# A fused attention and long-convolution kernel: a new written order of steps, PSUM pools and copy engines

## The chip, the core and the metric

The kernel runs on one core of a Trainium2 chip. Its time is device microseconds of one launch, taken by the device. The core's engines work beside each other, each through its own queue in order: TensorE (PE, with its weight loads as PEld), VectorE (DVE), ScalarE (ACT), GpSimd (POOL) and SyncE (SP), which here issues nearly all DMA transfers. A profile comes from one execution of its own, whose time can differ from the median of the timed runs.

## The reference

Two independent parts share the sequence length S = 2048 and the width D = 576; their outputs stand side by side in 1152 columns, all in bf16.

```python
# part A: dilated sliding attention, H = 32 heads of 18 columns, window W = 8, dilation 2
qkv = x @ wqkv                                  # [2048, 3*576]
logits[h, s, w] = q[h, s] . k[h, s - 2*w] / sqrt(18)     # -1e9 where s - 2*w < 0
attn = softmax(logits over w)
o[h, s] = sum_w attn[h, s, w] * v[h, s - 2*w]
a = o @ wo
# part B: short and long convolution (H3)
k_shift = sum_t shift(k, t) * shift_k[:, t]     # 4 taps
kv = k_shift * v
y = irfft(rfft(kv, 4096) * rfft(ssm_k, 4096))[:2048] + kv * ssm_D
out = concat(a, q * y)
```

## The kernel before

Part A keeps x, q, k and v transposed, so heads lie on partitions. Part B does the long transform in two matmul stages with a transposition through DRAM between them: stage one writes `Dx` (from kv) and `Dk` (from the filter), stage two reads them back in eight groups (two halves of the columns, four groups of rows), multiplies the spectra, inverts, writes `Dy`, and a last stage reads `Dy`.

Nothing schedules this program at run time. One string, `ORDER`, lists 405 steps, and a loop (last lines of the kernel function) calls the function of each step in turn, so each engine's queue holds its instructions in just this order. A step's letter after the colon picks a PSUM pool (`a` or `b`, two buffers each) and the engine of the copy out of PSUM (`s`: ACT, L103; `v`: DVE, L105). Without a letter the step's default holds; a `ys` without `s` multiplies straight out of PSUM on DVE. Before an instruction the tile framework puts the waits its data need. Each SP transfer also waits for the one about eight places ahead of it to land, since eight semaphores go round.

The steps, with their functions' lines:

| step | what it does |
|---|---|
| `lx` L234, `lwq`, `lwt`, `lwv` L247-L258 | load x in half quarters (288 KB each), and the weights |
| `lk` L241, `lv` L238, `ld` L268 | load k in four chunks (`lk.0` also two halo pieces), v in four, ssm_D |
| `lkn` L260, `kw` L264, `kt` L476 | load the filter by DMA transpose into a ring of seven, write it as rows to `Kt`, read it back in eight pieces |
| `tj`, `t0` to `t5`, `tv`, `tw` L284-L358 | constants; `t3` ends in a sine on ACT that `tw` on DVE needs |
| `wm` L291 | eleven matmuls on zeros |
| `ia`, `ib` L411, L423; `im` L416 | transposed tables by DMA; a negated table by a copy |
| `xt` L365, `sk` L445 | transpose x on PE; spread the four taps over partitions |
| `qk` L395, `qt` L401, `wt` L442 | projections for q and k; their tails; a copy of weight columns |
| `cv` L453 | short convolution on DVE, eight instructions per chunk (L455, L461, L468) |
| `sx`, `kp` L426 | stage one of kv and filter: two matmuls, a copy, and after each third two stores to `Dx` or `Dk` |
| `v` L379 | v projection, 40 matmuls |
| `lm` L484, `lb` L493 | products q times shifted k on DVE; sum over a head's columns on PE |
| `sm` L512 | softmax in two halves |
| `kl`, `xl` L546, `ks`, `xs` L536 | load and transform one group |
| `gp` L559, `gi` L568 | spectrum product on DVE; inverse on PE, then a POOL store to `Dy` |
| `pm` L584, `ps` L591 | weights times shifted v on DVE; their sum on PE |
| `po` L622, `pz` L627 | output projection; `pz` holds the last two `ps` |
| `yl` L635, `ql` L639, `ys` L643 | load `Dy` and q, last transform, product, store |

Intermediate results live in rings that a step takes a slot from and a later one gives back. The full products of `lm` have three slots; `lb.n` gives two back:

```python
prr = Ring(*[mk.take(2, S) for _ in range(3)])                         # L224
nc.vector.tensor_tensor(prr.get((n, h)), q2[h], k2[h][...], ALU.mult)   # L487, lm.n.h
prr.drop((n, 0)); prr.drop((n, 1))                                      # end of lb.n
```

The output stages of `ys` have two slots (L229), the loaded groups four (L216).

Of the kernel before, what the change touches and what calls it, by code (L numbers as in the profile page):

```python
# [15 lines left out]


ORDER = """
tj lx.0.0 lx.0.1 lx.2.0 lwq.1.0 lx.1.0 lx.2.1 lwt lx.1.1 lwq.1.1 lwq.0.1 tv lk.0 lx.3.0 t2 sk.0:a t0 lk.2 sk.2:bv
lx.3.1 sk.1:b xt.0.1:bs xt.0.0:as xt.0.2:bs wm.11:a xt.2.2:as t3 xt.1.2:bs xt.1.0:as qk.1.0.0:b lk.1 xt.2.1:as  # L20
xt.1.1:as xt.2.0:bs t1 tw lwq.0.0 cv.0.0 cv.0.1 t4 qk.1.1.0:b wt qk.1.1.1:a t5 lv.0 lwv lkn.8 lkn.2 lkn.12 lkn.9 lk.3
lkn.13 lkn.4 qk.1.1.2:b xt.3.2:bs qk.0.1.0:a cv.0.3 lkn.6 xt.3.1:bs lkn.7 cv.0.4 lkn.5 lv.1 kw.6 cv.0.2 cv.0.5
xt.3.0:as cv.1.4 cv.0.6 cv.1.0 qk.0.0.2:b cv.1.1 kw.4 lkn.10 cv.0.7 kw.3 qk.0.1.2:b cv.1.3 lkn.14 qk.0.0.1:a sx.0.0:a
sx.0.1:b cv.3.3 cv.1.2 qk.1.1.3:b lkn.15 lkn.0 sx.0.2:a cv.1.5 sx.1.0:a lkn.11 qk.0.1.3:b cv.3.4 sx.1.1:b qt.3:a lkn.1
sx.1.2:b cv.2.1 kw.7 lkn.3 ld qk.0.1.1:a qt.0:b cv.1.6 cv.2.3 kw.0 kw.5 cv.2.4 cv.1.7 qk.0.0.3:b cv.2.0 cv.2.2
sx.2.0:a cv.2.5 kw.2 kw.1 qt.2:b cv.3.5 sx.2.1:a cv.2.6 sx.2.2:b kt.0 cv.3.1 qk.1.0.2:a sx.3.0:b sx.3.1:a kt.1
sx.3.2:b cv.3.0 qt.1:a qk.0.0.0:b qk.1.0.1:a qk.1.0.3:b kp.0.0:a lv.2 cv.3.2 lm.0.2 cv.3.6 kp.0.1:b lm.6.2 lv.3
kp.0.2:a lm.6.1 kp.1.0:b lm.6.0 cv.2.7 kp.1.1:b kp.1.2:a lm.0.0 v.4:a lb.6:a kt.3 kt.2 sx.4.0:b sx.4.1:a lm.0.1 lm.7.0
ia.3 sx.4.2:a sx.5.0:b sx.5.1:b v.2:a ia.5 lb.0:a ia.1 sx.5.2:b kp.2.0:b kt.4 cv.3.7 kp.2.1:a vz kp.2.2:a kt.7 lm.7.1
ia.0 lm.1.0 v.7:b lb.7:b lm.4.1 sx.6.0:a ib sx.6.1:a sx.6.2:b v.1:b sx.7.0:a lm.1.1 sx.7.1:b lm.2.2 sx.7.2:b lb.1:a  # L30
ia.2 lm.4.2 kp.7.0:a lm.4.0 kp.7.1:b xl.3 kp.7.2:b lm.2.1 v.5:a lb.4:b kt.6 kp.3.0:b lm.2.0 kp.3.1:a lm.3.0 kp.3.2:b
im.0 v.3:a kt.5 xl.5 lb.2:b kp.4.0:a kp.4.1:b kp.4.2:b lm.3.1 xl.6 im.1 v.6:a lb.3:a ia.7 kp.6.0:a kp.6.1:b lm.5.0
kp.6.2:a kp.5.0:b lm.5.1 lb.5:av kp.5.1:a sm.1.0 sm.1.1 kp.5.2:b sm.1.2 sm.1.3 xs.5.0:a sm.1.4 xs.3.0:bv ia.4 sm.0.0
v.0:a vh.1 sm.0.1 sm.1.5:a sm.0.2 xs.5.1:a sm.0.3 sm.0.4 xs.3.1:b v.8:a sm.1.6 pm.1.0 pm.1.6 kl.3 sm.0.5:a ps.1.0:b
ks.3.0:a pm.1.3 vh.0 ks.3.1:b gp.3.0 kl.5 gp.3.1 sm.0.6 ps.1.6:a kl.2 ks.5.0:b ks.5.1:a ps.1.3:b pm.0.0 lwo.0 xl.2
kl.0 ks.2.0:a vh.2 ks.2.1:b ia.6 xl.0 lwo.3 gi.3.0:a gi.3.1:b ps.0.0:a gp.5.0 xs.2.0:b gi.5.0:a gp.5.1 pm.1.1 gi.5.1:b
gp.2.0 pm.1.4 xs.2.1:b gp.2.1 ks.0.0:a pm.0.3 xs.6.0:b xl.1 gi.2.0:a ks.0.1:b kl.6 ql.1 xs.0.0:a xs.0.1:b kl.1 lwo.1
gp.0.0 gi.2.1:a ps.1.1:b gp.0.1 ps.0.3:a pm.0.8 xs.1.0:b pm.0.7 gi.0.0:a ks.6.0:b xs.6.1:a kl.7 ps.1.4:bv gi.0.1:a
ks.1.0:b pm.0.1 ks.6.1:a gp.6.0 xl.4 ps.0.7:b gp.1.0 ps.0.8:b ql.3 pm.0.4 xs.1.1:a ks.1.1:b gi.6.0:a ps.0.1:b kl.4
gi.1.0:a gp.6.1 gp.1.1 pm.1.5 pm.0.6 ks.7.0:b xl.7 ql.2 lwo.2 xs.4.0:a gi.1.1:b ps.0.4:a ql.0 ks.4.0:b gi.6.1:a pm.0.5  # L40
xs.7.0:b ps.1.5:av xs.7.1:b ks.7.1:a yl.2 xs.4.1:b ps.0.5:a ps.0.6:b gp.7.0 ks.4.1:a yl.3 yl.1 gi.7.0:b gp.4.0
gi.4.0:a pm.0.2 gp.4.1 yl.0 ps.0.2:b gp.7.1 gi.4.1:a gi.7.1:bv ys.2.0:as ys.2.1:b ys.3.0:as ql.4 ys.3.1:a pm.1.2 yl.4
ql.7 po.0.0.0:v pm.1.8 yl.7 pm.1.7 po.0.1.0 ps.1.2:a ys.0.0:bs ys.0.1:as po.0.0.1:v yl.6 pz.1.0.0 ys.4.0:as ql.6
ys.4.1:as ys.1.0:bs ys.1.1:a ql.5 yl.5 po.1.0.1:v po.1.1.0 ys.7.0:b ys.6.0:as ys.7.1:as ys.6.1:b po.1.1.1:v po.0.1.1
ys.5.0:a ys.5.1:bs
"""


# [654 lines left out]
```

## Time and profile before

| | |
|---|---|
| runs, median (lowest to highest) | 210.17 us (209.7 to 215.51), 3 runs |
| the profiled execution | 211.04 us, span 209.1 us |
| busy in the span | PE 185.2 us (89%), PEld 118.3 (57%), DVE 177.8 (85%), ACT 160.7 (77%), POOL 12.9 (6%) |
| transfers | 56.20 MB, mean 269 GB/s |
| chain that ended last | PE 46%, ACT 27%, DMA 16%, issue 6%, DVE 2% |
| granted TensorE clock | full in all 40 slices |

Busy shares are means over stretches with different limits: PE is nearly always busy in the first 60 us and in the last 35, DVE from 15 to 170 us, ACT most between 105 and 170. Line L103 is the copy helper on ACT, used by nearly every step, so rows are told apart by tile and shape. A row of a window gives the busy time of each engine in it, with the number of instructions in brackets. In a group's row, the numbers behind the bar are the busy time of the group, the mean duration of one in ns, and the idle time of its engine just before, with what ended most of it.

### The profile page before, as it was taken

The numbers are of one execution on the slowest core, as the hardware profiler recorded it, in microseconds if no ns is written. First come the engines' busy times: TensorE is split into PE (matmuls) and PEld (weight loads), VectorE is DVE, ScalarE is ACT, GpSimd is POOL, SyncE is SP. The second block draws the span as 40 slices with busy tenths as digits, with TensorE's granted clock in tenths as the row PEclk, the third lists the DMA queues.
The fourth block names the chain that finished last, engine by engine and source line by source line (L and its number), as shares of the span: only waits on it lengthen the run. The fifth ranks groups of instructions, "written<-read, shape, count | busy, mean of one in ns | idle before, by whom it ended". The sixth has DMA issues, their size and how long they took to land.

```text
span 209.1 us, 6223 instructions
## 1 busy us (share of the span) xinstructions
PE 185.2 (89%) x2645; PEld 118.3 (57%) x2645; DVE 177.8 (85%) x157; ACT 160.7 (77%) x244; POOL 12.9 (6%) x39
## 2 busy tenths in 40 slices
...
GB/s 162 317 316 396 239 211 158 311 198 299 275 368 247 260 181 261 241 214 367 261 250 226 264 242 240 310 350 246 256 390 246 179 330 377 248 335 304 223 314 135
DMA packets 66797, 56.20 MB, mean 269 GB/s; under 512 B 16673, under 2 KB 60306, under 8 KB 66770
## 3 DMA queue, kind: packets, MB, share of 16 engines
...
q8 instruction: 20, 0.33, 0.7%
...
q10 hardware_dynamic: 2, 0.00, 0.0%
...
## 4 chain that ended last, share of the span: by engine, by line
PE 46%; ACT 27%; DMA 16%; issue 6%; DVE 2%; SPq 0%; ACTq 0%; DVEq 0%
ACT area L103 24%; PE psB L377 8%; PE psA L377 5%; DMA Dx<-area 5%; PE psA L610 5%; DMA out_dram<-area 4%; DMA Dy<-area 4%; PE psA L384 3%; PE psA L576 3%; PE psB L599 3%; PE psB L432 2%; DMA Dk<-area 2%; PE psA L599 2%; PE psA L432 2%; DMA area<-in_B_shift_k_dram 2%
## 5 line engine op out<-in xcount | busy, mean ns | idle before, releaser
L103 ACT ACTIVATE area<-psA 128x576 bf16<-128x576 f32 (+7 forms) x117 | 83.5, 757 | 33.1 <-PE psB L610 15.0
L103 ACT ACTIVATE area<-psB 128x576 bf16<-128x576 f32 (+5 forms) x113 | 80.2, 757 | 7.9 <-PE psB L377 4.0
L588 DVE TENSOR_TENSOR area<-area,area 128x4096 bf16<-128x4096 bf16 x18 | 40.6, 2284 | 0.9 <-DMA area<-area 0.8
L487 DVE TENSOR_TENSOR area<-area 128x4096 bf16<-128x4096 bf16 x16 | 35.8, 2286 | 1.0 <-PE psA L504 0.7
L377 PEld LDWEIGHTS <-area 128*128 128x128 bf16 x160 | 15.5, 98 | 17.5
L377 PE MATMUL psB<-area,area 128*128 128x512 bf16 x100 | 23.1, 379 | 0.0
L563 DVE TENSOR_TENSOR area<-area 128x2304 bf16<-128x2304 bf16 x16 | 21.1, 1351 | 1.3 <-ACT area L103 1.0
L461 DVE TENSOR_TENSOR area<-area,area 128x2304 bf16<-128x2304 bf16 x16 | 21.0, 1348 | 0.0
L541 PEld LDWEIGHTS <-W 128*64 128x64 bf16 x256 | 14.0, 108 | 12.3 <-issue 11.1
L610 PE MATMUL psA<-area,area 32*128 32x288 bf16 x288 | 18.7, 281 | 1.6 <-ACT area L103 1.1
L610 PE MATMUL psB<-area,area 32*128 32x288 bf16 x288 | 18.7, 281 | 0.0
L384 PEld LDWEIGHTS <-area 128*32 128x32 bf16 x360 | 15.2, 142 | 5.6 <-issue 2.8
L599 PEld LDWEIGHTS <-ident 64*64 64x64 bf16 x576 | 15.3, 106 | 5.1 <-issue 3.5
L610 PEld LDWEIGHTS <-area 32*128 32x128 bf16 x576 | 15.5, 93 | 4.6 <-issue 2.2
L384 PE MATMUL psA<-area,area 128*32 128x512 bf16 x280 | 16.7, 384 | 0.4 <-ACT area L103 0.2
L432 PEld LDWEIGHTS <-T 128*128 128x128 bf16 x96 | 8.6, 97 | 14.6 <-issue 9.3
L541 PE MATMUL psB<-area,W 128*64 128x288 bf16 x152 | 14.7, 290 | 1.8 <-ACT area L103 1.1
L455 DVE TENSOR_TENSOR area<-area,area 128x2304 bf16<-128x2304 bf16 x12 | 15.8, 1350 | 0.1
L576 PEld LDWEIGHTS <-IAt 64*128 64x128 bf16 x256 | 12.4, 94 | 5.8 <-issue 1.5
L432 PE MATMUL psB<-area,T 128*128 128x384 bf16 x52 | 12.6, 326 | 3.5 <-ACT area L103 3.5
L377 PE MATMUL psA<-area,area 128*128 128x512 bf16 x60 | 13.9, 379 | 0.0
L576 PE MATMUL psA<-area,IAt 64*128 64x288 bf16 x176 | 13.0, 283 | 0.4
...
## 6 DMA issues: line engine op xcount, KB each, us to landing
...
```

Source lines behind the costliest of these rows:

```text
L103: nc.scalar.activation(dst, src, ACT.Copy, **({} if scale is None else {"scale": scale}))
L377: nc.tensor.matmul(ps[:, u, :], w[:, kb, cols[u]:cols[u] + 128], xT[:, j, kb], start=(kb == 0), stop=(kb == 4))
L384: nc.tensor.matmul(ps[32 * a:32 * a + 32, u, :], wv[:, kb, 2 * n + u:D:DH], xT[:, a, kb], start=(kb == 0), stop=(kb == 4), tile_position=( ...
L432: nc.tensor.matmul(ps[:, ri, 0:384], T1[:, ri, :], sf[:, 384 * ch:384 * ch + 384], start=True, stop=not extra)
L461: nc.vector.tensor_tensor(dst, kfull[:, 4 * c + 3 - j:4 * c + 7 - j, :], skb[:, j, :].unsqueeze(1).to_broadcast([128, 4, D]), ALU.mult)
L487: nc.vector.tensor_tensor(prr.get((n, h)), q2[h], k2[h][:, :, o0:o0 + S], ALU.mult)
L541: nc.tensor.matmul(ps[64 * hp:64 * hp + 64, im, 0:HD], W2[:, im, 8 * g + 2 * prl + hp].rearrange("p l f -> p (l f)"), Wt[:, 2 * prl + hp, ...
L563: nc.vector.tensor_tensor(Pv, Xv.unsqueeze(2).to_broadcast([128, 2, 2, 2 * HD]), Kv.unsqueeze(1).to_broadcast([128, 2, 2, 2 * HD]), ALU.mult)
L576: nc.tensor.matmul(ps[:, hp, 0:HD], IAt[r, tab, 4 * g + 2 * hv + u, :], Pp[(i, hv)][r, n, u, :], start=(n == 0), stop=(n == 3), tile_posit ...
L588: nc.vector.tensor_tensor(Pr.get((hv, p)), vv, Lt[:, :, 256 * hv:256 * hv + 256].unsqueeze(2).to_broadcast([128, W, 2, 256]), ALU.mult)
L599: nc.tensor.matmul(ps[64 * b:64 * b + 64, r, 0:256], ident[g, g], P[g, n, :, 128 * b:128 * b + 128], start=(n == 0), stop=(n == W - 1), ti ...
L610: nc.tensor.matmul(pss[e][:, b, 0:HD], Os[hv][g, d // 2, r, 128 * (d % 2):128 * (d % 2) + 128], wo4[g, d, d0:d1], start=(d == 0), stop=(d ...
```

## The change

Only the string `ORDER` differs. It holds the same 405 steps, so all instructions of PE, all transfers and all memory areas are the same; their sequence on each engine, the pool of many PSUM tiles, and the copy engine of some steps differ. On DVE instead of ACT are now the copies of `xt.2.0`, `xt.0.1`, `sx.2.2`, `im.0`, `kp.5.2`, `v.0`, `xs.0.0`, `ps.0.2` and `po.0.1.0`; back on ACT are those of `sk.2`, `lb.5`, `xs.3.0`, `ps.1.4`, `ps.1.5`, `gi.7.1`, one in `pz`, and of `po.0.0.1`, `po.1.0.1`, `po.1.1.1`, while `po.0.1.1` goes to DVE; seven instead of ten `ys` go by ACT. The string was searched anew, under eight sets of disturbed transfer times. Cut to the parts that the prediction speaks of:

```diff
-tj lx.0.0 lx.0.1 lx.2.0 lwq.1.0 lx.1.0 lx.2.1 lwt lx.1.1 lwq.1.1 lwq.0.1 tv lk.0 lx.3.0 t2 sk.0:a t0 lk.2 sk.2:bv
-lx.3.1 sk.1:b xt.0.1:bs xt.0.0:as xt.0.2:bs wm.11:a xt.2.2:as t3 xt.1.2:bs xt.1.0:as qk.1.0.0:b lk.1 xt.2.1:as
-xt.1.1:as xt.2.0:bs t1 tw lwq.0.0 cv.0.0 cv.0.1 t4 qk.1.1.0:b wt qk.1.1.1:a t5 lv.0 lwv lkn.8 lkn.2 lkn.12 lkn.9 lk.3
-lkn.13 lkn.4 qk.1.1.2:b xt.3.2:bs qk.0.1.0:a cv.0.3 lkn.6 xt.3.1:bs lkn.7 cv.0.4 lkn.5 lv.1 kw.6 cv.0.2 cv.0.5
-xt.3.0:as cv.1.4 cv.0.6 cv.1.0 qk.0.0.2:b cv.1.1 kw.4 lkn.10 cv.0.7 kw.3 qk.0.1.2:b cv.1.3 lkn.14 qk.0.0.1:a sx.0.0:a
-sx.0.1:b cv.3.3 cv.1.2 qk.1.1.3:b lkn.15 lkn.0 sx.0.2:a cv.1.5 sx.1.0:a lkn.11 qk.0.1.3:b cv.3.4 sx.1.1:b qt.3:a lkn.1
-sx.1.2:b cv.2.1 kw.7 lkn.3 ld qk.0.1.1:a qt.0:b cv.1.6 cv.2.3 kw.0 kw.5 cv.2.4 cv.1.7 qk.0.0.3:b cv.2.0 cv.2.2
-sx.2.0:a cv.2.5 kw.2 kw.1 qt.2:b cv.3.5 sx.2.1:a cv.2.6 sx.2.2:b kt.0 cv.3.1 qk.1.0.2:a sx.3.0:b sx.3.1:a kt.1
-sx.3.2:b cv.3.0 qt.1:a qk.0.0.0:b qk.1.0.1:a qk.1.0.3:b kp.0.0:a lv.2 cv.3.2 lm.0.2 cv.3.6 kp.0.1:b lm.6.2 lv.3
-kp.0.2:a lm.6.1 kp.1.0:b lm.6.0 cv.2.7 kp.1.1:b kp.1.2:a lm.0.0 v.4:a lb.6:a kt.3 kt.2 sx.4.0:b sx.4.1:a lm.0.1 lm.7.0
-ia.3 sx.4.2:a sx.5.0:b sx.5.1:b v.2:a ia.5 lb.0:a ia.1 sx.5.2:b kp.2.0:b kt.4 cv.3.7 kp.2.1:a vz kp.2.2:a kt.7 lm.7.1
...
-kp.6.2:a kp.5.0:b lm.5.1 lb.5:av kp.5.1:a sm.1.0 sm.1.1 kp.5.2:b sm.1.2 sm.1.3 xs.5.0:a sm.1.4 xs.3.0:bv ia.4 sm.0.0
-v.0:a vh.1 sm.0.1 sm.1.5:a sm.0.2 xs.5.1:a sm.0.3 sm.0.4 xs.3.1:b v.8:a sm.1.6 pm.1.0 pm.1.6 kl.3 sm.0.5:a ps.1.0:b
...
-xs.7.0:b ps.1.5:av xs.7.1:b ks.7.1:a yl.2 xs.4.1:b ps.0.5:a ps.0.6:b gp.7.0 ks.4.1:a yl.3 yl.1 gi.7.0:b gp.4.0
-gi.4.0:a pm.0.2 gp.4.1 yl.0 ps.0.2:b gp.7.1 gi.4.1:a gi.7.1:bv ys.2.0:as ys.2.1:b ys.3.0:as ql.4 ys.3.1:a pm.1.2 yl.4
-ql.7 po.0.0.0:v pm.1.8 yl.7 pm.1.7 po.0.1.0 ps.1.2:a ys.0.0:bs ys.0.1:as po.0.0.1:v yl.6 pz.1.0.0 ys.4.0:as ql.6
-ys.4.1:as ys.1.0:bs ys.1.1:a ql.5 yl.5 po.1.0.1:v po.1.1.0 ys.7.0:b ys.6.0:as ys.7.1:as ys.6.1:b po.1.1.1:v po.0.1.1
-ys.5.0:a ys.5.1:bs
+lx.2.1 lx.2.0 lx.3.0 lx.3.1 tj t0 wm.11:a t2 lx.0.1 xt.2.2:bs xt.2.1:bs xt.3.2:as tv sk.0:b lx.0.0 xt.0.0:bs lx.1.1 t3
+ld xt.2.0:b lx.1.0 sk.1:a xt.0.1:a xt.1.0:bs sk.2:a xt.1.1:bs lwt xt.3.0:as xt.1.2:bs lwq.0.1 qk.0.1.2:a lk.0
+xt.0.2:as xt.3.1:bs lwq.0.0 tw cv.0.0 cv.0.1 t4 lwv cv.0.4 cv.0.3 lwq.1.0 cv.0.2 lwq.1.1 cv.0.5 lk.1 wt cv.1.1 cv.0.6
+cv.1.0 ia.7 lv.1 lv.0 cv.0.7 cv.1.4 lkn.0 lkn.6 lkn.7 cv.1.3 cv.1.2 lk.2 cv.1.5 cv.2.4 cv.1.6 cv.2.3 qk.0.1.1:b
+qk.0.1.0:a qk.1.1.0:b cv.1.7 qk.1.1.3:a cv.2.1 lkn.12 cv.2.5 lk.3 cv.3.4 lkn.10 qk.1.1.1:a lkn.13 qk.0.1.3:b sx.0.0:a
+lkn.8 lv.2 lkn.14 sx.0.1:a kw.3 lkn.9 lkn.15 qk.0.0.2:b sx.0.2:b sx.1.0:a qk.1.0.0:a lkn.4 t1 kw.6 lkn.1 sx.1.1:b
+qk.1.1.2:a sx.1.2:a cv.3.3 cv.2.0 cv.3.5 t5 lkn.5 cv.2.2 lkn.2 qk.0.0.1:b kw.7 lkn.11 sx.2.0:a qk.0.0.0:a cv.3.1 kw.0
+lkn.3 kw.2 kw.4 ia.0 sx.2.1:b qt.2:b kw.5 qk.0.0.3:a kw.1 sx.3.0:b sx.2.2:bv cv.2.6 qt.0:a kt.0 qt.3:b kt.1 sx.3.1:a
+sx.3.2:a qk.1.0.3:b cv.3.0 cv.2.7 cv.3.2 qt.1:a lm.6.2 cv.3.6 qk.1.0.1:a lm.0.2 qk.1.0.2:b lv.3 kt.2 kp.0.0:b lm.6.1
+lm.6.0 kp.0.1:b kp.0.2:b lm.7.0 kp.1.0:a kp.1.1:b ia.2 kp.1.2:a v.2:b lb.6:b ia.6 sx.4.0:a sx.4.1:a kt.7 lm.0.0
+sx.4.2:b v.4:b lm.0.1 sx.5.0:b sx.5.1:a kt.3 sx.5.2:a lb.0:b kp.2.0:a cv.3.7 lm.7.1 ia.3 lm.1.1 ia.1 kp.2.1:a kp.2.2:b
...
+kp.7.0:b ib lm.2.0 lm.2.2 kp.7.1:a kp.7.2:a v.1:b lb.4:a lm.2.1 kp.3.0:a xl.6 kp.3.1:b kp.3.2:b v.6:a lm.3.1 lb.2:a vz
+lm.3.0 lm.5.0 kt.6 kp.4.0:b kp.4.1:a kp.4.2:b v.3:a kt.5 lb.3:b im.1 lm.5.1 v.5:a xl.5 kp.6.0:b im.0:v lb.5:a sm.1.0
+sm.1.1 xl.3 sm.1.2 sm.1.3 ql.2 kp.6.1:b sm.0.0 kp.6.2:a kp.5.0:a kp.5.1:b kp.5.2:bv sm.0.1 v.0:av sm.0.2 sm.0.3 vh.1
...
+ql.1 pm.0.2 xs.4.1:a ks.4.0:b xs.7.0:a yl.3 gp.4.0 yl.2 ps.0.5:b ps.0.2:av xs.7.1:b gp.7.0 yl.1 ks.4.1:a yl.0 gi.4.0:b
+gp.7.1 gi.7.0:a gp.4.1 pm.1.2 ql.0 pm.1.8 gi.7.1:b gi.4.1:a ys.3.0:bs ys.2.0:as ps.1.2:b ys.3.1:a ys.2.1:b po.0.0.0:v
+ql.6 yl.4 pm.1.7 ql.4 yl.6 po.0.0.1 ys.0.0:a ys.0.1:b po.0.1.0:v yl.7 pz.1.0.0:s ys.4.0:a ys.4.1:b ys.1.0:a ys.1.1:bs
+ql.7 po.1.1.0 yl.5 po.1.0.1 ys.6.0:a ys.6.1:bs ql.5 ys.7.0:as ys.7.1:b po.1.1.1 po.0.1.1:v ys.5.0:bs ys.5.1:as
```

In words, where the two differ most: all of x is loaded first; `wm` and `t0` come before other preparation; the second chunk of weights comes after `lk.0`; the v loads come before most `lkn`; tables `ia.7` and `ia.0` and load `lv.2` stand ahead of `kt.0`; `cv.2.7` comes before the `lm` steps; and near the end `gi.4.1` is the last of the inverses, `ps.1.2` comes before the first `po`, and `ys.6` is done before `ys.7`.

More of the change, by code (lines that the diff above doesn't have):

```diff
@@ L29 @@
-ia.3 sx.4.2:a sx.5.0:b sx.5.1:b v.2:a ia.5 lb.0:a ia.1 sx.5.2:b kp.2.0:b kt.4 cv.3.7 kp.2.1:a vz kp.2.2:a kt.7 lm.7.1
-ia.0 lm.1.0 v.7:b lb.7:b lm.4.1 sx.6.0:a ib sx.6.1:a sx.6.2:b v.1:b sx.7.0:a lm.1.1 sx.7.1:b lm.2.2 sx.7.2:b lb.1:a
-ia.2 lm.4.2 kp.7.0:a lm.4.0 kp.7.1:b xl.3 kp.7.2:b lm.2.1 v.5:a lb.4:b kt.6 kp.3.0:b lm.2.0 kp.3.1:a lm.3.0 kp.3.2:b
-im.0 v.3:a kt.5 xl.5 lb.2:b kp.4.0:a kp.4.1:b kp.4.2:b lm.3.1 xl.6 im.1 v.6:a lb.3:a ia.7 kp.6.0:a kp.6.1:b lm.5.0
-kp.6.2:a kp.5.0:b lm.5.1 lb.5:av kp.5.1:a sm.1.0 sm.1.1 kp.5.2:b sm.1.2 sm.1.3 xs.5.0:a sm.1.4 xs.3.0:bv ia.4 sm.0.0
@@ L34 @@
-v.0:a vh.1 sm.0.1 sm.1.5:a sm.0.2 xs.5.1:a sm.0.3 sm.0.4 xs.3.1:b v.8:a sm.1.6 pm.1.0 pm.1.6 kl.3 sm.0.5:a ps.1.0:b
[L35 to L38, printed above, removed]
@@ L39 @@
-ks.1.0:b pm.0.1 ks.6.1:a gp.6.0 xl.4 ps.0.7:b gp.1.0 ps.0.8:b ql.3 pm.0.4 xs.1.1:a ks.1.1:b gi.6.0:a ps.0.1:b kl.4
-gi.1.0:a gp.6.1 gp.1.1 pm.1.5 pm.0.6 ks.7.0:b xl.7 ql.2 lwo.2 xs.4.0:a gi.1.1:b ps.0.4:a ql.0 ks.4.0:b gi.6.1:a pm.0.5
-xs.7.0:b ps.1.5:av xs.7.1:b ks.7.1:a yl.2 xs.4.1:b ps.0.5:a ps.0.6:b gp.7.0 ks.4.1:a yl.3 yl.1 gi.7.0:b gp.4.0
-gi.4.0:a pm.0.2 gp.4.1 yl.0 ps.0.2:b gp.7.1 gi.4.1:a gi.7.1:bv ys.2.0:as ys.2.1:b ys.3.0:as ql.4 ys.3.1:a pm.1.2 yl.4
-ql.7 po.0.0.0:v pm.1.8 yl.7 pm.1.7 po.0.1.0 ps.1.2:a ys.0.0:bs ys.0.1:as po.0.0.1:v yl.6 pz.1.0.0 ys.4.0:as ql.6
```

8 lines of the change are left out of this document (added).

## The prediction, made before the changed kernel ran

> **What bounds the kernel now.** I read the profiled execution first by stretches, cut where the leading work changes: preparation, the shifted convolution (`cv`), the attention logits (`lm`, `lb`), the long mixed part (`pm`, `gp`, copies), the output part, and the last store. Columns after the stretch: busy time of PE, PE weight load, DVE, ACT, POOL, then the granted clock, the DMA share and GB/s.
>
> ```profile
> 0.00:17.20 17.20, 11.34 (x86) 7.36 (x87) 9.29 (x29) 10.36 (x14) 5.89 (x27) 1.00 0.92 274
> 17.20:58.90 41.70, 41.35 (x215) 19.87 (x213) 40.71 (x34) 34.82 (x45) 0.33 (x1) 1.00 1.06 260
> 58.90:106.20 47.30, 41.82 (x541) 23.54 (x538) 43.86 (x27) 39.99 (x54) 0.89 (x1) 1.00 0.98 265
> 106.20:171.80 65.60, 60.44 (x1076) 43.76 (x1074) 61.69 (x42) 63.83 (x113) 4.75 (x8) 1.00 0.98 270
> 171.80:204.10 32.30, 30.26 (x738) 23.79 (x736) 21.10 (x28) 10.95 (x19) 1.06 (x2) 1.00 1.02 300
> ```
>
> No one engine bounds it. From 17.2 to 171.8 us DVE is busy 146.3 of 154.6 us; ACT works 63.8 of the 65.6 us of the fourth stretch; PE carries the output part, 30.3 of 32.3. The DMA engines are near full throughout. A new order can only move the start of these rows and fill the few gaps, so I look at the gaps next: the groups of DVE with the idle time before them, and what ended it.
>
> ```profile
> L588 DVE TENSOR_TENSOR area<-area,area 128x4096 bf16<-128x4096 bf16 x18 | 40.6, 2284 | 0.9 <-DMA area<-area 0.8
> L487 DVE TENSOR_TENSOR area<-area 128x4096 bf16<-128x4096 bf16 x16 | 35.8, 2286 | 1.0 <-PE psA L504 0.7 <-PE psB L504 0.4
> L563 DVE TENSOR_TENSOR area<-area 128x2304 bf16<-128x2304 bf16 x16 | 21.1, 1351 | 1.3 <-ACT area L103 1.0 <-issue 0.2
> L343 DVE TENSOR_TENSOR W<-area 128x2048 bf16<-128x2048 bf16 x2 | 2.4, 1220 | 3.8 <-ACT area L337 3.8
> ```
>
> The big rows hardly wait. The one long wait, 3.8 us, stands before `tw` (L343): DVE waits there for the sine of `t3` on ACT, and `cv.0.0` follows `tw`. From there to the last `gp` (L563) DVE runs from 17.15 to 170.52 us, 153.4 us, of which 144.8 are work (end-to-end spacing of its rows) and 8.6 are a dozen small waits. So I follow DVE up to the last `gp` and PE from there to the end.
>
> **The start.** The old queue has 2768 KB ahead of `lk.0` (six half loads of x at 288, weights of 256, 144, 320 and 320 KB), the new one 2769 KB (eight halves, 144, 320 and the 1 KB of `ld`). So `lk.0` should land when it does now, at 14.66 us by the trace's landing records, and its halo pieces at 16.1 and 16.3. Now nothing uses it until 17.15, because `tw` came late. In the new order on ACT, four copies (0.6, 1.02, 0.6, 1.02) and `xt.0.0` stand ahead of that sine; `xt.0.0` needs two halves that land fifth and sixth, some 9.4 us by the present landings, so the sine ends near 12. `tw` then stands on DVE behind the copies of `xt.2.0` and `xt.0.1`, new there (between 0.4 us, the row of 512 int32 elements, L335, and 1.02, ACT's row for the same copy; I take 0.6), and ends near 14.3. ACT has `sk.2`, which `cv.0.0` also reads, done by about 14.2. `cv.0.0` then waits for `lk.0` and starts at about 15.2: **-1.95 us** (bounds -2.5, at the landing, and 0, if ACT's copies slip).
>
> `wm` moves ahead of all other PE work. The first 20 transposes now take 2.1 us (from 7.73 to the first `wm` at 9.87, 0.107 each); 16 at 15.83 take 0.9 (0.056). After the move they should run at the short pitch. I price this at nothing, because those copies wait for x and ACT.
>
> **DVE work.** Between `cv.0.0` and the last `gp` DVE loses the copies of `lb.5`, `xs.3.0`, `ps.1.4`, `ps.1.5` (0.69 + 1.50 + 0.69 + 0.68 = 3.56 us). It gains `xs.0.0` (1.50), `ps.0.2` (0.69), `sx.2.2` and `kp.5.2` (768 columns: 512 take 0.69 and 576 take 0.75, so 0.94 each), `v.0` (1024 columns, 1.19) and `im.0` (2048 columns; between 0.69, the L336 row with 1024, and 1.22, L491 with 2048; I take 0.9): 6.16. Less 0.08 overlap for each of two more rows that is **+2.5 us**. ACT gets the difference back, but in the fourth stretch, where it is tightest, it does not: from `sm.1.4` to the last `gi` its rows add up to 64.0 us in the new order and 62.4 in the old. No gain is booked there.
>
> **The transfers ahead of `kt.0`.** The new SP queue has `lv.2` (576 KB) and two of the `ia` transposes (128 KB each) ahead of `kt.0`. At 260 GB/s (second stretch) 832 KB are 3.3 us; by SP's issue time, about 1.25 us a transpose and 0.5 for the load, 3.0; without `ld`'s 0.46 and other shifts I get 2.3 to 3.3. `kt.0` lands now at 58.64, then at about 61.3. These are the present rows around it, SP, PE, DVE:
>
> ```profile
> 51.98 1.57 SPq L439 DMA_DIRECT2D Dx<-area  x2
> 55.26 0.81 SPq L477 DMA_DIRECT2D area<-Kt  x2
> ```
> ```profile
> 59.41 0.33 PE L432 MATMUL psA<-area,T 128*128 128x384 bf16 x1
> 65.28 1.04 PE L504 MATMUL psA<-area,Eh 128*32 128x512 bf16 x16
> 66.25 0.50 PE L432 MATMUL psB<-area,T 128*128 128x384 bf16 x2
> ```
>
> `kp.0.0` (59.41) needs `kt.0`; `lb.6` (ends at 66.32) stands behind it on PE. The new PE queue reaches `kp.0.0` sooner: first projection at about 14.3 (its copy slot waits for `sk.2`) to 16.5, then 15 `qk` x 2.16, 4 `qt` x 1.08, 12 `sx` x 0.33 and two `xt`, 41.4 us, so 57.9. It waits to 61.5, and `lb.6` ends after 5.4 us of rows, at 66.9. The products of `lm` live in a ring of three; `lm.6.1`, `lm.6.0`, `lm.7.0` fill it, and `lm.0.0` must wait for `lb.6`. DVE is there at 15.2 + 49.4 + 0.5 = 65.1, so it stalls 1.8 us. (The old order has `cv.2.7` in this place, 1.27 us of cover that is now gone.) Idle up to here is 2.3 us against 1.3: **+1.0 us**, bounds -0.8 (lands in time) and +4.5.
>
> **The rest.** The remaining 7.3 us of DVE gaps I keep; they come from many waits of under 1.2 us, and the new order has others. Bounds: 3 and 12. After the last `gi` both orders have the same 30 us of PE rows and a last store, and the second-half `yl` have some 16 us of PE work to land behind. `ys.5.0` now waits for a store's landing; `ys.6` done first takes that wait away. But `ys.5.1` is then held by ACT, whose rows at the end are as many: 0.
>
> Sum: -1.95 + 2.5 + 1.0 = +1.55 on the profiled execution's own 211.04 us (span 209.1 and 1.9 around it): 212.6. That execution stands 0.87 above the median of the runs shown, 210.17, so I forecast **211.8 us**.
>
> **Rivals.**
> *Slower: `kt.0` comes much later.* Place: SP, in order. For it: the old queue loses 1.7 us just before `kt.0` waiting for the rows' landing, and SP waits 17.2 us in all for ACT before stores; two stores stand right before `kt.0` in both orders. Against: SP was never far behind there. From a landing after 64 us the whole gives 2%: `lb.6` ends at 69.6, DVE idle 5.0, so -1.95 + 2.5 + 3.7 = +4.25. Landing at 65.5 costs 1.5 more: 216 us on the scale of the median.
> *Slower still: the pace of PE falls.* If PE idles over 6 us there, `v.2` and `lb.6` behind the gap may run at the long pitch that the first rows show: 3.4 us of rows become 6.8, 219 us. Against it: the longest gap after the start is 1.40 us and shows nothing of the kind, so no row tells from what length on. [...]
> *Faster: the lead is kept and gaps close.* For it: `lk.0`'s landing is a firm bound, and ACT has 3.8 us fewer copies up to the softmax. With DVE gaps of 3.5 instead of 8.6: -1.95 + 2.5 - 5.1 = -4.55, 205.6. Against: twelve different waits would all have to shrink.
>
> **How the numbers follow.** Two per cent (206.0 to 214.4 us) is about what a measurement of this kernel can tell from no change. Forecast 0.55, late `kt.0` 0.27, lost pace 0.04, faster 0.14; the two slower ones together give 0.31. The range takes in the late `kt.0` and, below, the bounds of the gaps: 205.5 to 217 us.
>
> **What would show it.** `cv.0.0` near 15.2 us; `kt.0` landing near 61 with PE waiting before `kp.0.0`; a DVE gap of about 2 us before `lm.0.0`, released by PE; the last `gp` about 1.5 us later than 170.5; about 38.5 us from there to the end. Wrong if `cv.0.0` starts after 17, if the gap before `lm.0.0` is none or over 4.5 us, or if DVE's gaps after it leave 3 to 12 us.

## The result and the profile after

| | before | after |
|---|---|---|
| median of 4 runs each | 210.89 us | 218.06 us (217.07 to 218.47) |
| ratio, 95% interval | 1 | **1.0353** (1.0277 to 1.0428) |
| profiled execution, span | 211.04, 209.1 us | 218.25, 216.5 us |
| last `gp` ends; from there to the end of the span | 170.52; 38.6 us | 178.24; 38.3 us |

The changed kernel is 7.4 us slower (0.0353 x 210.9), outside the predicted range of 205.5 to 217 us. Ratios leave disturbed executions out, so those of `e1`, `e4` and `g2` rest on two of four runs, and since the profiled executions of `e1`, `f4`, `g2` and `g3` were disturbed, only the ratio is used for these four. Below, "+2.6 us" is a ratio times 210.9. Line numbers of the changed kernel are one lower than before.

The changed kernel by stretches, cut at the steps that the prediction used (`cv.0.0`, first `lm`, end of the first softmax, last `gp`); columns as in the prediction:

```profile
0.00:14.90 14.90, 11.42 (x89) 6.50 (x91) 11.64 (x30) 10.42 (x14) 5.75 (x27) 1.00 0.91 267
14.90:58.90 44.00, 42.52 (x208) 19.86 (x209) 42.93 (x35) 33.18 (x44) 0.33 (x1) 1.00 1.12 274
58.90:105.60 46.70, 41.48 (x546) 23.05 (x550) 42.20 (x26) 37.80 (x52) 0.89 (x1) 1.00 1.00 259
105.60:178.20 72.60, 60.91 (x1055) 41.94 (x1044) 63.02 (x44) 64.10 (x113) 4.76 (x8) 0.95 0.87 237
178.20:216.50 38.30, 31.64 (x752) 24.94 (x752) 20.03 (x26) 14.12 (x24) 1.07 (x2) 0.96 0.98 283
```

The first three stretches end at 105.6 us, 0.6 earlier than before (106.2). The fourth holds the loss. The prediction's row for it reaches to 171.8, 1.3 us beyond the last `gp`; cut at 170.5, the old stretch is 64.3 us long, with 62.7 us of ACT and 61.3 of DVE. So the new one is 8.3 us longer for 1.4 us more work on ACT and 1.8 on DVE; the rate has dropped to 237 GB/s and the granted clock is below 1. The groups of DVE, with the idle time before them, point to the spectrum product:

```profile
L587 DVE TENSOR_TENSOR area<-area,area 128x4096 bf16<-128x4096 bf16 x18 | 40.6, 2286 | 0.9 <-PE psB L598 0.4 <-DMA area<-area 0.4
L486 DVE TENSOR_TENSOR area<-area 128x4096 bf16<-128x4096 bf16 x16 | 35.8, 2286 | 2.6 <-PE psB L503 1.2 <-PE psA L503 1.2
L562 DVE TENSOR_TENSOR area<-area 128x2304 bf16<-128x2304 bf16 x16 | 21.5, 1355 | 7.8 <-PE psA L575 3.9 <-ACT area L102 3.1 <-PE psB L575 0.6
L342 DVE TENSOR_TENSOR W<-area 128x2048 bf16<-128x2048 bf16 x2 | 2.4, 1222 | 0.1
```

`tw` (L342) has lost its 3.8 us wait. But `gp` (L562) waits 7.8 us where it waited 1.3: 3.9 us once, for PE, and 3.1 us in several waits for ACT copies. The three places on DVE that matter, in its timeline:

```profile
14.88 1.36 DVE L460 TENSOR_TENSOR area<-area,area 128x2304 bf16<-128x2304 bf16 x1 [0.92 <-DMA area<-in_B_k_dram]
...
66.79 4.50 DVE L486 TENSOR_TENSOR area<-area 128x4096 bf16<-128x4096 bf16 x2 [1.18 <-PE psB L503]
...
133.11 1.36 DVE L562 TENSOR_TENSOR area<-area 128x2304 bf16<-128x2304 bf16 x1 [3.90 <-PE psA L575]
```

The first two are the announced signs (`cv.0.0` and `lm.0.0`); the third is new, `gp.2.0`. Two steps of DVE cut the rest: the first product `pm.1.0` ends at 113.54 (114.34 before), `gp.0.1` at 146.72 (140.61), the last `gp` at 178.24 (170.52). From `pm.1.0` to `gp.0.1` the new order takes 33.18 us against 26.27 (+6.9), from there to the last `gp` 31.52 against 29.91 (+1.6). With the lead of 0.8 that is the whole 7.7 us by which the last `gp` is late.

What stands around the long wait, first on PE:

```profile
124.76 0.68 PE L540 MATMUL psA<-area,W 128*64 128x288 bf16 x8
129.79 1.17 PE L540 MATMUL psB<-area,W 128*64 128x288 bf16 x8 [4.35 <-DMA area<-Dx]
130.90 2.10 PE L575 MATMUL psA<-area,IAt 64*128 64x288 bf16 x16
132.93 1.92 PE L598 MATMUL psB<-area,ident 64*64 64x256 bf16 x32
134.78 1.34 PE L575 MATMUL psA<-area,IAt 64*128 64x288 bf16 x16
```

PE stands 4.35 us before `xs.2.0`, which needs the load of group 2, `xl.2`. Behind it in PE's queue are `gi.3.1`, `ps.1.6` and `gi.5.1`, which don't need that load. DVE's 3.90 us before `gp.2.0` end with `gi.3.1` (L575), so that wait is this one handed on, and `pm.1.1` queues behind it. Then the loads, on SP:

```profile
113.99 0.34 SPq L271 DMA_DIRECT2D area<-in_A_wo_dram  x1
117.73 0.33 SPq L546 DMA_DIRECT2D area<-Dx  x1
118.12 0.43 SPq L271 DMA_DIRECT2D area<-in_A_wo_dram  x1
```

`xl.2` is issued at 117.73 (before: 117.29) and lands at 129.75, after 12.0 us (7.9). The output weights `lwo.0` stand ahead of it, as before; but `lwo.3`, which the old order issued at 123.19, now comes 0.4 us behind it. The windows of 5 us show what that does, first after, then before:

```profile
120.00:125.00 5.00, 4.54 (x83) 3.03 (x80) 4.53 (x4) 5.00 (x10) 0.00 (x0) 1.00 1.01 182
125.00:130.00 5.00, 0.65 (x10) 0.32 (x8) 4.21 (x3) 1.90 (x4) 0.00 (x0) 0.84 1.05 184
130.00:135.00 5.00, 5.00 (x60) 2.81 (x58) 1.46 (x2) 2.59 (x5) 0.58 (x1) 0.50 0.72 215
```
```profile
120.00:125.00 5.00, 4.73 (x80) 3.43 (x79) 4.18 (x4) 5.00 (x10) 0.00 (x0) 1.00 1.40 256
125.00:130.00 5.00, 3.75 (x72) 2.72 (x73) 5.00 (x4) 4.67 (x10) 0.58 (x1) 1.00 0.81 226
```

The DMA engines count as fully busy (share 1.01 and 1.05) and move 182 and 184 GB/s. After the gap the clock of PE is 0.50 for 5 us, and the steps in it take longer: `gi.3.1` 2.10 us, where the `gi` rows of the old order at this place take 1.14 to 1.21.

### The profile page after: what moved, and what is told of

Its sections match the earlier page's. It is cut to its first block, busy times and chain, and to the rows that moved or that the text cites. A ratio compares the mean times of both kernels' runs of the same rounds, so it can differ in the third digit from the quotient of the medians.

```text
span 216.5 us, 6205 instructions
## 1 busy us (share of the span) xinstructions
PE 188.0 (87%) x2640; PEld 116.3 (54%) x2645; DVE 179.8 (83%) x155; ACT 159.6 (74%) x243; POOL 12.8 (6%) x39
## 4 chain that ended last, share of the span: by engine, by line
PE 35%; DMA 31%; ACT 17%; SPq 9%; issue 4%; DVE 2%; ACTq 0%; DVEq 0%
ACT area L102 15%; DMA area<-Dx 9%; DMA area<-in_A_wqkv_dram 7%; SPq L261 4%; PE psB L598 4%; PE psA L383 3%; PE psA L376 3%; PE psB L376 3%; DMA out_dram<-area 3%; PE psA L575 3%; DMA Dx<-area 3%; PE psA L609 3%; DMA area<-in_B_q_dram 2%; PE psB L431 2%; DMA area<-in_A_x_dram 2%
## 5 line engine op out<-in xcount | busy, mean ns | idle before, releaser
L102 ACT ACTIVATE area<-psA 128x576 bf16<-128x576 f32 (+7 forms) x112 | 77.4, 731 | 28.5 <-PE psB L609 9.0
L102 ACT ACTIVATE area<-psB 128x576 bf16<-128x576 f32 (+7 forms) x118 | 82.3, 734 | 18.7 <-PE psB L540 4.8
L562 DVE TENSOR_TENSOR area<-area 128x2304 bf16<-128x2304 bf16 x16 | 21.5, 1355 | 7.8 <-PE psA L575 3.9
L540 PEld LDWEIGHTS <-W 128*64 128x64 bf16 x256 | 13.9, 110 | 18.4 <-issue 12.3
L460 DVE TENSOR_TENSOR area<-area,area 128x2304 bf16<-128x2304 bf16 x16 | 21.3, 1354 | 1.2 <-DMA area<-in_B_k_dram 1.1
L540 PE MATMUL psB<-area,W 128*64 128x288 bf16 x144 | 14.0, 300 | 7.9 <-DMA area<-Dx 5.6
L376 PE MATMUL psA<-area,area 128*128 128x512 bf16 x87 | 20.6, 379 | 0.2
L609 PEld LDWEIGHTS <-area 32*128 32x128 bf16 x576 | 16.1, 93 | 3.9 <-issue 2.1
L383 PEld LDWEIGHTS <-area 128*32 128x32 bf16 x360 | 14.1, 141 | 6.6 <-issue 2.8
L376 PE MATMUL psB<-area,area 128*128 128x512 bf16 x69 | 16.0, 379 | 0.5 <-DMA area<-in_A_wqkv_dram 0.5
L575 PEld LDWEIGHTS <-IAt 64*128 64x128 bf16 x256 | 12.2, 97 | 7.3 <-issue 2.8
L454 DVE TENSOR_TENSOR area<-area,area 128x2304 bf16<-128x2304 bf16 x12 | 16.0, 1352 | 0.0
L431 PE MATMUL psB<-area,T 128*128 128x384 bf16 x48 | 11.3, 326 | 3.5 <-DMA area<-Kt 1.8
L575 PE MATMUL psA<-area,IAt 64*128 64x288 bf16 x160 | 13.0, 302 | 0.3 <-ACT area L102 0.2
L540 PE MATMUL psA<-area,W 128*64 128x288 bf16 x112 | 10.5, 289 | 2.7 <-DMA area<-Dk 1.5
## 6 DMA issues: line engine op xcount, KB each, us to landing
area<-in_A_wo_dram SPq DMA_DIRECT2D x4, 648.0 KB, 12.5
```

Source lines behind the costliest of these rows:

```text
L102: nc.scalar.activation(dst, src, ACT.Copy, **({} if scale is None else {"scale": scale}))
L376: nc.tensor.matmul(ps[:, u, :], w[:, kb, cols[u]:cols[u] + 128], xT[:, j, kb], start=(kb == 0), stop=(kb == 4))
L383: nc.tensor.matmul(ps[32 * a:32 * a + 32, u, :], wv[:, kb, 2 * n + u:D:DH], xT[:, a, kb], start=(kb == 0), stop=(kb == 4), tile_position=( ...
L431: nc.tensor.matmul(ps[:, ri, 0:384], T1[:, ri, :], sf[:, 384 * ch:384 * ch + 384], start=True, stop=not extra)
L460: nc.vector.tensor_tensor(dst, kfull[:, 4 * c + 3 - j:4 * c + 7 - j, :], skb[:, j, :].unsqueeze(1).to_broadcast([128, 4, D]), ALU.mult)
L540: nc.tensor.matmul(ps[64 * hp:64 * hp + 64, im, 0:HD], W2[:, im, 8 * g + 2 * prl + hp].rearrange("p l f -> p (l f)"), Wt[:, 2 * prl + hp, ...
```

## The experiments

The theory: the loss is one wait, `xs.2.0` for `xl.2`, and a smaller one late; the rivals are the new first half, the lost clock, and the bytes rather than the kind of the loads.

**Which half.** `e3` runs the new order up to `pm.1.0` and the old one behind it; `e4` the reverse.

```diff
 e3: new order ... sm.1.6 pm.1.0 | then all steps not yet done, in the old order
 e4: old order ... sm.1.6 pm.1.0 | then all steps not yet done, in the new order
```

> The new order up to pm.1.0, then the remaining steps in the old order. Theory (the loss is made wholly after pm.1.0; up to there the new order is 0.8 us ahead, pm.1.0 ends at 113.54 against 114.34): 209 to 211 us, as before or up to 1 us under. Rival (the new first half hands on a debt, Dk stores and kl loads 2 us later, that costs more than its lead): 212 to 215.

> The old order up to pm.1.0, then the remaining steps in the new order. Theory (the loss sits in the order of the second half, lwo.0 and lwo.3 around xl.2): 217 to 220 us with a wait of over 3 us before xs.2.0. Rival (it takes the new first half, with its late kl loads, to make xl.2 late): 211 to 214.

`e3` measured 1.0019 (0.9973 to 1.0066), the same as before; `e4` 1.0172 (1.0071 to 1.0274), +3.6 us. So the first half costs nothing and the second half costs time also behind the old first half, but only half of the 7.4: in `e4` `xl.2` lands after 9.4 us and PE waits 1.9 us for it, under the 3 us expected. This size is rough, as the four runs of `e4` lie between 212.8 and 218.1 us. The size of the stall hangs on how the second half meets the landing times. The lead of the new first half could have come through in `e3`. It did not: `kl.2` was issued at 117.79 only, the DMA moved 57 GB/s from 115 to 120 us, and `gp.0.0` waited 2.5 us.

`f4` pulls that load forward in `e3`.

```diff
-xs.5.1:a sm.0.4 ... kl.2
+xs.5.1:a kl.2 sm.0.4 ...
```

> The order made of the new first half and the old second half (which ran like the kernel before), with kl.2 moved up behind xs.5.1, so that it takes the buffer that xs.5 frees and not the one of ks.3. Theory (in that mixed order kl.2 was issued at 117.79 us against 111.86 in the old one, transfers stood nearly still from 115 to 120 us, and the later xl.0 made gp.0.0 wait 2.5 us): kl.2 issued near 112, no wait over 1 us before gp.0.0, 208 to 210 us, under both kernels. Rival (the lead of the first half is lost to ACT, which is full): 210 to 211.

1.0018 (0.9968 to 1.0069): no gain over `e3`. The late `kl.2` alone did not hold the lead back.

**The stall.** `e1` moves the load `lwo.3` behind `xl.0`, `e2` moves the steps that need `xl.2` behind those that don't, `f1` does both.

```diff
 e1, f1
-xl.2 lwo.3 ks.5.0:a ... gp.5.1 xl.0 pm.1.4
+xl.2 ks.5.0:a ... gp.5.1 xl.0 lwo.3 pm.1.4
 e2, f1
-xs.2.0:b vh.2 gi.3.1:a gp.2.0 ps.1.6:b gi.5.1:a pm.1.1 xs.2.1:a
+vh.2 gi.3.1:a ps.1.6:b gi.5.1:a pm.1.1 xs.2.0:b gp.2.0 xs.2.1:a
```

> The new order with one load moved: lwo.3 (648 KB of the output weights) is issued behind xl.0 instead of right behind xl.2. Theory (the stall at xs.2.0 comes from xl.2 sharing the transfers with lwo.3): xl.2, issued near 117.7 us, lands near 126 instead of 129.75, PE waits under 1 us before xs.2.0, the granted clock stays full, and the time falls by 3 to 5 us from 218.1, to 213 to 215. Rival one (the order of the second half is too long for ACT and DVE, the stall only takes up slack that is lost anyway): the landing is earlier but the time stays at 217 to 218. Rival two (xl.2 is late because the Dk stores and the kl loads before it run 2 us late): landing within 1 us of 129.75, time 217 to 218.

> The new order with xs.2.0 moved behind gi.3.1, ps.1.6, gi.5.1 and pm.1.1, and gp.2.0 behind it; all transfers as in the new order. Theory (PE, which works in order, stands behind xs.2.0 with other work ready, loses 4.4 us there and then its clock for some 6 us): PE does 3.5 us of rows in the gap, DVE has pm.1.1 (2.2 us) in it, the clock stays full, time 213 to 215. Rival (the landing of xl.2 alone sets what follows, since gp.2.0, gi.2.0 and the rest of group 2 hang on it): 216.5 to 218.

> The new order with both moves at once: lwo.3 behind xl.0, and xs.2.0 with gp.2.0 behind pm.1.1. Each alone gave 214.4. Theory (both take away the same stall, the wait of PE and DVE for xl.2, so they overlap, and what is left over the old kernel is made after gp.0.1): 212.5 to 214.5 us, no wait over 1.5 us on PE between 120 and 135 us. Rival (two separate losses, which add): 210 to 211.5.

`e1` 1.0125 (1.001 to 1.024), `e2` 1.0211 (1.0126 to 1.0296), `f1` 1.0103 (1.0014 to 1.0193). In microseconds the loss of 7.4 falls to 2.6, 4.5 and 2.2, near the theory each time; the intervals of `e1` and `f1` don't part these two. PE around `xs.2.0` in `f1`:

```profile
123.91 1.21 PE L575 MATMUL psA<-area,IAt 64*128 64x288 bf16 x16 [0.85 <-ACT area L102]
125.05 1.07 PE L598 MATMUL psB<-area,ident 64*64 64x256 bf16 x32
126.05 1.15 PE L575 MATMUL psA<-area,IAt 64*128 64x288 bf16 x16
127.13 0.68 PE L540 MATMUL psB<-area,W 128*64 128x288 bf16 x8
```

`gi.3.1`, `ps.1.6` and `gi.5.1` come first, at the short pitch, and `xs.2.0` (127.13) finds `xl.2` landed at 122.42. From `pm.1.0` to `gp.0.1` `f1` takes 26.91 us, 0.6 above before. So one transfer moved and two steps moved take away 5.3 of the 7.4 us (0.025 x 210.9), with the rest of the new order in place.

**The lost clock.** `f2` puts 16 matmuls on constants into the gap, so that PE doesn't idle.

```diff
-pm.1.4 xs.2.0:b
+pm.1.4 wf.16:b xs.2.0:b        # 16 matmuls of 512 columns into a tile nobody reads
```

> The new order with 16 matmuls of 512 columns on constants (3.4 us at the short pitch) ahead of xs.2.0, in the gap in which PE waits for xl.2; nothing reads their result. Theory (after that gap the granted clock is 0.50 for some 5 us, and xs.2.0, gi.3.1, ps.1.6 take twice as long, 2.2 us more): clock stays full, these rows run at 0.68, 1.15 and 1.07 us, time falls by 1.5 to 2.5 us to 215.5 to 216.5. Rival (DVE waits for the landing of xl.2 anyway, so PE's pace costs nothing): full clock and 217.5 to 218.5.

```profile
127.67 3.61 PE L298 MATMUL psB<-W,ident 128*128 128x512 bf16 x16
132.18 0.68 PE L545 MATMUL psB<-area,W 128*64 128x288 bf16 x8 [0.90 <-DMA area<-Dx]
132.80 1.15 PE L580 MATMUL psA<-area,IAt 64*128 64x288 bf16 x16
```

The filling (3.61 us) leaves a gap of 0.90, and behind it `gi.3.1` takes 1.15 us, not 2.10. Yet the ratio is 1.0349 (1.0288 to 1.0409), as after. In this profile the way from `pm.1.0` to `gp.0.1` is 2.4 us shorter than in the changed kernel's (30.79), but this execution came to `pm.1.0` 2.3 us later. One profile each and medians of four can't part these, so the price of the slow 5 us stays between 0 and 2.4 us; the wait itself would remain in any case.

**The late part.** `f3` runs the old order up to `gp.0.1` and the new one behind it.

```diff
 f3: old order ... ps.1.1:b gp.0.1 | then all steps not yet done, in the new order
```

> The old order up to gp.0.1, then the new one. Theory (part of the loss is made after gp.0.1, without xl.2: gp.6.1 waits for a slot that gi.1.0 gives back, and in the new order ps.0.1, ps.0.4 and ks.7.0 stand ahead of gi.1.0 on PE): 1.5 to 3 us over the kernel before, 212 to 214, with a wait of about 1 us before gp.6.1. Rival (the whole loss is the stall at xl.2 and its clock): 210 to 211.3.

1.0064 (1.0021 to 1.0107), +1.3 us. DVE's timeline in `f3` behind `gp.0.1`, its rows that wait:

```profile
142.15 2.29 DVE L587 TENSOR_TENSOR area<-area,area 128x4096 bf16<-128x4096 bf16 x1 [1.03 <-PE psA L598]
...
155.58 1.36 DVE L562 TENSOR_TENSOR area<-area 128x2304 bf16<-128x2304 bf16 x1 [0.73 <-ACT area L102]
...
164.45 1.36 DVE L562 TENSOR_TENSOR area<-area 128x2304 bf16<-128x2304 bf16 x1 [0.90 <-ACT area L102]
166.13 0.69 DVE L104 CAST area<-psA 128x512 bf16<-128x512 f32 x1 [0.32 <-PE psA L598]
...
168.49 2.63 DVE L562 TENSOR_TENSOR area<-area 128x2304 bf16<-128x2304 bf16 x2 [0.41 <-ACT area L102]
```

The longest, 1.03 us before `pm.0.7` just behind the join, does not stand in the changed kernel. The other four do (0.95, 0.90, 0.32 and 0.41 us before `gp.6.1`, `gp.4.0`, the copy of `ps.0.2` and `gp.7.1`). Of these all but the third end with an ACT copy out of PSUM, so not with the slot that my expectation named. They are the best candidate for the other loss, the 1.6 us from `gp.0.1` on, but `f3` does not part them from what the join itself costs.

`g3` tries to use both findings: `f1` up to `gp.0.1`, the old order behind it.

```diff
 g3: f1 ... gp.0.1 | then all steps not yet done, in the old order
```

> The new order with lwo.3 and xs.2.0 moved (211.8 us) up to gp.0.1, then the old order. Theory (two separate losses, the stall at xl.2 and 1.4 us of DVE waits for ACT copies after gp.0.1): both gone, 209.5 to 211, at or just under the kernel before. Rival (the lead of 1.8 us that the mended order has at gp.0.1 is kept): 208 to 209.

1.0069 (1.0027 to 1.0111): missed, no better than `f3`. A likely reason, not shown, is that two orders joined at a step leave each other's loads at places that were not meant for them.

**Why `xl.2` lands so late.** `g1` moves both weight loads away from it, `g2` leaves them and moves two other loads (864 KB) away.

```diff
 g1
-kl.2 lwo.0 vh.0 ... xl.2 lwo.3 ... xl.0 pm.1.4 ... xl.1 xs.0.1:a
+kl.2 vh.0 ... xl.2 ... xl.0 lwo.0 pm.1.4 ... xl.1 lwo.3 xs.0.1:a
 g2
-kl.0 gp.5.0 ks.2.0:a gi.5.0:b ql.3 ... xl.0 pm.1.4
+gp.5.0 ks.2.0:a gi.5.0:b ... xl.0 kl.0 ql.3 pm.1.4
```

> The new order with both loads of output weights out of the way of xl.2: lwo.0 behind xl.0 and lwo.3 behind xl.1; xs.2.0 stays where the new order has it. Theory (these loads hold up xl.2): it lands within 7 us of its issue (12.0 in the new order, 8.9 with lwo.3 alone moved), PE does not wait for it over 0.5 us, and the time is 1 to 3 us under the 214.4 of the single move, 211.5 to 213.5. Rival (any load of this size does it, and the transfers behind simply move up): landing 8 to 10 us after issue, 214 to 215.

> The new order with kl.0 (576 KB) and ql.3 (288 KB) behind xl.0, and lwo.0 and lwo.3 left around xl.2: more bytes moved away from behind xl.2 than by moving lwo.3 (648 KB). Theory (lwo is what slows it, not the bytes in flight): xl.2 still lands 11 to 12.5 us after its issue and the time stays at 217 to 218.5. Rival (bytes in flight): landing within 9 us, 214 to 215.

`g1` 1.0141 (1.0049 to 1.0234): `xl.2` lands after 3.8 us, `kl.0` after 4.9 instead of 13.6, and the way from `pm.1.0` to `gp.0.1` is 26.11 us, as before. So `xl.2` lands after 3.8 us with no weight load beside it, 6.3 to 7.9 with the one ahead (`f1`, `e3`, `f3` and before) and 9.4 to 12.1 with the other close behind it too (`e2`, `e4`, `f2` and the changed kernel). But `xl.1`, with two weight loads close behind it, takes 9.1 us and `xs.1.0` waits 1.7, and the late part takes 32.18 us instead of 31.52: part of the delay seems to go with these loads. `g2` 1.0185 (1.009 to 1.028), from runs between 213.1 and 219.2 us: I expected no gain, but by the ratio less traffic beside `xl.2` also helps, by about half.

Each of the four weight loads writes 648 KB into 32 partitions. `h1` (new order) and `h2` (old order) write the same weights with four loads into all 128 partitions, each a part of the rows, read four times over from a source with a leading repeat of four.

```diff
-nc.sync.dma_start(wo4[32 * g:32 * g + 32], A_wo.rearrange("(h d) n -> h d n", d=DH), ...)
+d0, d1 = ((0, 4), (8, 12), (12, 18), (4, 8))[g]
+src = A_wo.rearrange("(h d) n -> h d n", d=DH)[:, d0:d1, :]
+nc.sync.dma_start(wo4[:, d0:d1, :], bass.AP(tensor=src.tensor, offset=src.offset, ap=[[0, 4]] + [list(x) for x in src.ap]))
```

> The new order with the output weights loaded in another shape: each of the four lwo loads writes a quarter of the rows of d for all 128 partitions (576, 576, 864 and 576 KB) and not all of d for 32 partitions (648 KB each). The same 2592 KB, in the same places of the order. Theory (writing into 32 partitions only is what halves the transfers beside it): xl.2 lands within 7 us of its issue, lwo.0 and lwo.3 within 7, PE does not wait over 0.5 us before xs.2.0, time 211.5 to 214. Rival (the bytes of lwo are what hold up xl.2, whatever their shape): landing after 9 to 12 us, 216 to 218.

> The kernel before with its output weights loaded in the same other shape. Theory (its transfers from 113 to 133 us are held up by lwo as well, xl.2 lands after 7.9 us, but that is mostly covered): landing after 4 to 6 us, time 208.5 to 210.5, at or under the kernel before. Rival (a load of 128 partitions from a source that four groups share is slower, or other transfers suffer): 211 to 213.

1.0572 (1.0508 to 1.0637) and 1.0584 (1.0525 to 1.0643): far worse in both orders. These loads took 13 to 22 us to land, as the last update of each one's semaphore shows, and `xl.2` took 13.5 us in `h1`. The times say nothing about 32 partitions; the test replaced one slow form by a slower one. In the traces of `h1` and `h2`, behind one update 1 to 2 us after the issue, each semaphore shows just four more until the load has landed, where a weight load of the changed kernel shows 16. What makes this form so slow, no run shows.

`i1` (new order) and `i2` (old order) keep the total of 2592 KB and the places, and load plain rows of v into 128 partitions instead; the two loads around `xl.2` are then of 576 KB each instead of 648.

```diff
-nc.sync.dma_start(wo4[32 * g:32 * g + 32], A_wo.rearrange("(h d) n -> h d n", d=DH), ...)
+d0, d1, b0 = ((0, 4, 0), (8, 12, 8), (12, 18, 10), (4, 8, 4))[g]
+nc.sync.dma_start(wo4[:, d0:d1, :], vb16[:, b0:b0 + d1 - d0, :])
```

> The new order with the four loads of output weights replaced by plain loads of v into the same memory, in the same places: 576, 576, 576 and 864 KB, each for all 128 partitions with one run of bytes per partition. The output projection then multiplies with wrong weights; its work is the same. Theory (loads for 32 partitions only are what halves the transfers beside them): lwo.0 and lwo.3 land within 8 us of their issue, xl.2 within 7 (12.0 in the new order), PE does not wait over 1 us before xs.2.0, time 212 to 214.5. Rival (the bytes alone): xl.2 lands after 9 to 12 us, 216 to 218.

> The kernel before with the same replacement of the lwo loads (576 to 864 KB of v into all 128 partitions in place of 648 KB of wo into 32; the output projection multiplies with wrong weights). It is the control for the same edit in the new order, which came to 0.9959 of the kernel before. If the slow loads cost only the new order, because only that one puts its load of group 2 between two of them, the old order gains nothing: 0.995 to 1.005, its row before the loads' users unchanged. If the old order pays for them too, it gains 1 to 3 us (0.985 to 0.995), and then the new order would still be slower than the old one once both are rid of them. In the trace the old order's load of group 2 should land after 4 to 5 us instead of 7.9 in either case.

`i1` 0.9959 (0.9916 to 1.0002), a median of 210.1 us and so better than expected; `i2` 0.9935 (0.9882 to 0.9988). The same windows in `i1`:

```profile
120.00:125.00 5.00, 4.57 (x78) 3.13 (x71) 5.00 (x4) 5.00 (x11) 0.00 (x0) 1.00 0.91 300
125.00:130.00 5.00, 4.53 (x90) 3.29 (x91) 5.00 (x4) 5.00 (x10) 1.14 (x2) 1.00 0.59 226
```

300 GB/s instead of 182, and PE busy for 4.5 of 5 us in both windows. The page's rows of the transfers (KB each, us to landing), of the changed kernel and then of `i1`:

```profile
area<-Dx SPq DMA_DIRECT2D x8, 576.0 KB, 5.7
area<-Dk SPq DMA_DIRECT2D x8, 576.0 KB, 7.7
...
area<-in_A_wo_dram SPq DMA_DIRECT2D x4, 648.0 KB, 12.5
```
```profile
area<-Dx SPq DMA_DIRECT2D x8, 576.0 KB, 4.8
area<-Dk SPq DMA_DIRECT2D x8, 576.0 KB, 5.5
...
area<-in_B_v_dram SPq DMA_DIRECT2D x7, 576.0 KB, 5.9
```

The last row holds the four loads of v itself and three of those in the weights' place; the two around `xl.2` land after 5.8 and 6.1 us instead of 12.5 and 14.7, and `xl.2` after 4.6. The old order gains 1.4 us from this, the new one 8.3. So these loads cost both orders, but the new one six times as much, and without them the two differ by 0.5 us, less than the intervals can part. In these two profiles the last `gp` ends at 169.57 and 169.87.

The packet records of the traces, which the page only sums up, say more about the trait that matters. The weight loads move in packets of 2304 B, and in the changed kernel one took 195 ns (median of 1152; before, 186), while the 1024 packets of this size that read `Kt` into 128 partitions took 93. The 128 packets of 6912 B in `h2`, weights into 128 partitions, and in `i2`, v into 128 partitions, both took 262 ns. So packets of this size, or packets read from the weights, aren't slow in themselves, which points to the 32 partitions. And neighbours pay: packets of 4608 B, mostly at 178 ns, took 338 between 120 and 130 us of the changed kernel, beside two weight loads.

## Why the prediction was wrong

**The start** (-1.95, `cv.0.0` at 15.2): right; 14.88, so -2.3, with the wait for `lk.0` that was named.

**DVE work** (+2.5): right. Between `cv.0.0` and the last `gp`, DVE takes 163.4 us instead of 153.4: 2.3 more work and 7.7 more gaps (15.2 against 7.5 by adding them up, which the prediction had as 8.6). The forecast's terms for the work add up to 2.44 rather than 2.5, and its total to 211.7 rather than 211.8.

**The transfers ahead of `kt.0`** (+1.0): the mechanism was right and the idle time near, but the delay was half of the forecast. It lands at 59.94 (forecast 61.3, before 58.64); PE waits 1.81 us before `kp.0.0`; `lb.6` ends at 66.73 (66.9); DVE waits 1.18 us before `lm.0.0` (1.8). The rival that put a much later `kt.0` there did not happen.

**The rest** ("the remaining 7.3 us of DVE gaps I keep"): this step failed. Behind the wait at `lm.0.0` the gaps add up to 12.9 us, over the upper bound of 12 and over the 7.3 that were booked (in the old trace, added up in the same way, they are 6.5). I kept the number because the old waits were many and short, and followed the new order's transfers only up to `kt.0`. The old trace held what was needed: `xl.2` took 7.9 us with one weight load ahead of it, the median weight load took 10.2 us, and the new string has `xl.2 lwo.3` side by side and `xs.2.0` ahead of three PE steps that don't need it. The edit that mattered was one that I did not read. Removing it (`f1`) takes back 5.3 us; the late part behind the old order (`f3`) costs 1.3 us, the join included.

**ACT in the fourth stretch** (no gain booked for fewer copies): right as to the work, 64.1 us busy against 62.7 up to the last `gp`. But it became a loss: DVE waits 3.1 us for its copies before `gp`, where it waited 1.0.

**The end** (same 30 us of PE): right, 38.3 us against 38.6; the forecast was 38.5. As forecast, the last `ys` no longer waits for a store's landing; DVE now waits 4.48 us for one before `ys.6`, which did not lengthen the end.

**The rival of the lost pace** came about in another place. PE idled 4.35 us and the clock was 0.50 in the next 5 us, while gaps of 1.8 us left it full (1.81 in the changed kernel, 1.88 in `e4`). What a gap between these lengths does was not shown. At the start the column of the granted clock reads 1.00 although the first transposes of the old order ran at 0.107 us and later ones at 0.056, so it doesn't show every slow pace. But the loss was there first, as the wait, and `f2`, which kept the clock full, was no faster.

**What stays open.** The price of the slow clock (0 to 2.4 us); why the lead of 0.8 us from the first half never reached the end in `e3` and `f4`; and whether it is the 32 partitions alone that make the weight loads slow: `i1` changed the source and the packet size too, and only the packet times speak against these two. No version that loads the weights beat both kernels: `e3` and `f4` are level with before. The weights in a quick form that reaches all partitions were not found.
